# T5 attention and hash-routed experts in one kernel: zero fills, expert 0's head and the last chunk rescheduled

## The chip, the cores and the metric

One core of one Trainium2 chip. The metric is the device time of one execution in microseconds (us). The kernel before was timed three times; one more execution was taken with the profiler.

## What is computed

Attention with a relative-position bias over 8 batches of 8 heads, 576 positions of 64 values, then a mixture of 8 experts over the 4608 token rows of 512 values. A token's id decides its expert, so the assignment is known early, but its row of x is known only when attention has made it.

```python
scores = q @ k.transpose(0, 1, 3, 2) / sqrt(64) + bias_table[bucket]   # 8x8x576x576
attn   = softmax(scores)
x      = (attn @ v) as rows of 512                                     # 4608 rows
expert_idx = token_ids * 2654435761 % 8
for e in range(8):
    out[rows of e] = relu(x[rows of e] @ w1[e]) @ w2[e]                # 512 -> 1024 -> 512
```

## The kernel before

**Attention.** The work is 32 pairs of heads (`pairs`, four to a batch), each in five steps g = 0 to 4. For each step TensorE (PE) makes the scores of a pair in a PSUM slot (`products`, L475, and `add_bias`, L498; three slots, L174), ScalarE (ACT) takes their exponential into `att` (`scores`, L533), and the sum with v runs seven steps behind (`av_steps`, L601, nine matmuls a step, into the PSUM banks `aux0` and `aux1`). VectorE (DVE) multiplies two of the five `att` parts by a band factor (L543), divides the finished sums into `x_all` (L610, L611), copies the transposed k and q out of `aux1` (`transpose_qk`, L404 and L410) and casts v (`cast_v`, L252). GpSimd (POOL) casts q and k (L244).

**The order is written out by hand.** The loop at L853 takes the steps two at a time; `pair_start` (L784) issues what belongs to a pair's start, `behind` (L816) what comes after the scores. Each engine and each queue runs its instructions in that order and waits where an operand is not there. SyncE's queue (SP) issues the loads of q, k and v (L206, L220, L232), the routing's tables at pair 3, and the zero fills; POOL's queue issues the scatters and the weights' loads.

**From attention to the experts.** Expert e has 640 rows of a table `t_xperm` in device memory. `fill_table` (L746) writes zero rows with no token's id into the last 192 rows of each expert's share, 192 rows of 1028 bytes by one transfer, two experts a pair in pairs 4 to 7 (L794). From pair 10 on `send` lets POOL scatter finished rows of `x_all` to their places (`dispatch`, L625, five scatters a batch, two, two and one a pair). `route` (L306) works out the places and sets a flag where a count is out of bounds, so that a fallback behind the main part computes all rows.

**Heads.** The first 384 rows (`EARLY` x 128) of experts 0 and 1 are full before the last two batches, so they are read back early: `gather_head(0)` at the start of pair 29 into `xpn[0]`, `gather_head(1)` at the start of pair 31 (both L153, on SP). Weights of experts 0 and 1 are loaded by POOL at the starts of pairs 24, 26, 28 and 30 (`load_w1`, L140, and `load_w2`, L146), 1 MB each as they land. After the last pair `first_transpose` (L754, matmuls L760) transposes expert 0's head in a PSUM slot by 12 matmuls and one copy (L765), and 63 matmuls of the last two pairs' sums are left: 18 of pair 30, then 27 and 18 of pair 31.

**Experts.** The second part has pools of its own (`mo`, and `mop` in PSUM). Its parts (`PARTS`, L68) are the heads of experts 0 and 1, the rests of both, then experts 2 to 7 whole. For each, `first_layer` (L951 or L931) and a ReLU on ACT, then for each chunk of 128 rows `second_layer`: eight matmuls of 512 columns (L979), a copy by DVE (L985) and a scatter to the output (L986). The transposes of a later part stand between the chunks (`transpose_step`, L908 and L913).

Of the kernel before, what the change touches and what calls it, by code (L numbers as in the profile page):

```python
# [11 lines left out]
F32 = mybir.dt.float32  # L12
# [19 lines left out]
def kernel(  # L32
# [35 lines left out]
    PARTS = [(0, 0, EARLY), (1, 0, EARLY), (0, EARLY, NSC), (1, EARLY, NSC)]  # L68
    PARTS += [(e, 0, NSC) for e in range(2, E)]
    HEAD = (B - 2, B - 1)  # L70
    NPT = DM // P
    NFT = F // P
    NIT = 2 * NT + 1
# [25 lines left out]
    for t in range(NIT):  # L99
        for b in range(B):  # L100
# [22 lines left out]
    flag = cst.tile([1, 1], I32, name="flag")  # L123
    x_all = cst.tile([P, NRING, NIT, XW], F16, name="x_all")
    xpn = [cst.tile([P, c1 - c0, XW], F16, name=f"xpn_{e}_{c0}")
           for e, c0, c1 in PARTS[:4]]
    xpt0 = cst.tile([P, NPT, EARLY * P], F16, name="xpt0")
    w1t = [cst.tile([P, NPT, F], F16, name=f"w1t{i}") for i in range(2)]
    w2t = [cst.tile([P, NFT, DM], F16, name=f"w2t{i}") for i in range(2)]

# [35 lines left out]
    with tc.tile_pool(name="at", bufs=1) as at, tc.tile_pool(  # L166
# [139 lines left out]
        def route():  # L306
            name_rows(0, NRING)
            nc.vector.tensor_scalar(
                out=te[:, :, :KT].rearrange("p b (o t) -> p b o t", o=2),
                in0=ter[:, :, :, ::2].rearrange("p b t o -> p b o t"),  # L310
                scalar1=E - 1, scalar2=None, op0=ALU.bitwise_and,
            )
            nc.vector.tensor_scalar(
                out=te[:RC, :, KT:], in0=te[:RC, :, KT:], scalar1=E - 1,
                scalar2=None, op0=ALU.bitwise_and,
            )
            yield
            EN = E * NGT
            tef = te[:, :, :].rearrange("p b t -> p (b t)")
            oh = at.tile([P, E, NGT], F16, name="oh")  # L320
            nc.vector.tensor_tensor(
                out=oh[:, :, :],
                in0=tef.unsqueeze(1).to_broadcast([P, E, NGT]),
                in1=csts[:, NGT:].bitcast(F32).unsqueeze(2).to_broadcast(
                    [P, E, NGT]
                ),
                op=ALU.is_equal,
            )
            yield
            ohf = oh[:, :, :].rearrange("p e g -> p (e g)")  # L330
            rps = slot("rps")
            nc.tensor.matmul(out=rps[:, 0, :EN], lhsT=cnt[:, P:], rhs=ohf)
            nc.tensor.matmul(out=rps[:, 1, :EN], lhsT=cnt[:, :P], rhs=ohf)
            inc = at.tile([P, E, NGT], F32, name="inc")
            incf = inc[:, :, :].rearrange("p e g -> p (e g)")
            nc.vector.tensor_tensor_scan(
                out=incf, data0=keep[:, :, :].rearrange("p e g -> p (e g)"),
                data1=rps[:, 0, :EN], initial=0.0, op0=ALU.mult, op1=ALU.add,
            )
            yield  # L340
            rnk = at.tile([P, E, NGT], F32, name="rnk")
            rnkf = rnk[:, :, :].rearrange("p e g -> p (e g)")
            nc.vector.tensor_tensor(
                out=rnkf, in0=incf, in1=rps[:, 1, :EN], op=ALU.subtract
            )
            yield
            nc.vector.tensor_tensor(out=rnkf, in0=rnkf, in1=ohf, op=ALU.mult)
            yield
            rank = at.tile([P, NGT], F32, name="rank")
            nc.vector.tensor_reduce(  # L350
                out=rank[:, :], in_=rnk[:, :, :].transpose([0, 2, 1]),
                axis=mybir.AxisListType.X, op=ALU.add,
            )
            yield
            num = inc[:, :, NGT - 1]
            odd = at.tile([P, E + 2], F32, name="odd")
            nc.vector.tensor_scalar(
                out=odd[:, :E], in0=num, scalar1=float(LOW), scalar2=None,
                op0=ALU.is_lt,
            )  # L360
            nc.vector.scalar_tensor_tensor(
                out=odd[:, :E], in0=num, scalar=float(CAP), in1=odd[:, :E],
                op0=ALU.is_gt, op1=ALU.max,
            )
            yield
            for i, b in enumerate(HEAD):
                nc.vector.tensor_scalar(
                    out=odd[:, E + i : E + i + 1],
                    in0=inc[:, i, b * NIT - 1 : b * NIT],
                    scalar1=float(EARLY * P), scalar2=None, op0=ALU.is_lt,  # L370
                )
            bad = at.tile([P, 1], F32, name="bad")
            nc.vector.tensor_reduce(
                out=bad[:, :], in_=odd[:, :], axis=mybir.AxisListType.X,
                op=ALU.max,
            )
            yield
            sel = at.tile([P, NGT], F32, name="sel")
            nc.vector.scalar_tensor_tensor(
                out=sel[:, :], in0=tef, scalar=float(CAP), in1=rank[:, :],  # L380
                op0=ALU.mult, op1=ALU.add,
            )
            dlt = at.tile([P, NGT], F32, name="dlt")
            nc.vector.scalar_tensor_tensor(
                out=dlt[:, :], in0=tok, scalar=float(NSLOT),
                in1=sel[:, :], op0=ALU.add, op1=ALU.subtract,
            )
            yield
            nc.vector.scalar_tensor_tensor(
                out=ds2[:, :], in0=dlt[:, :], scalar=bad[:, :],  # L390
                in1=sel[:, :], op0=ALU.mult, op1=ALU.add,
            )
            nc.vector.tensor_copy(out=flag[:, :], in_=bad[:1, :])
            yield
# [230 lines left out]
        def dispatch(b, t):  # L625
# [8 lines left out]
                oob_is_err=False,  # L634
            )
            disjoint(sc_in, "xrows")
            for b0, read in heads:
                if b >= b0:
                    tc.declare_no_dep(
                        sc_in.ins, read.ins,  # L640
                        reason="the first rows of the list are of earlier "
                        "batches, or every row goes behind the lists",
                    )

        heads = []

        def gather_head(i):
            heads.append((HEAD[i], gather(i, xpn[i])))
# [96 lines left out]

        def fill_table(e):  # L746
            rows = CAP - LOW
            nc.sync.dma_start(
                out=xperm_d.ap()[CAP * (e + 1) - rows : CAP * (e + 1), :]
                .rearrange("(p r) d -> p (r d)", p=rows // 2),  # L750
                in_=zx[: rows // 2, :, :].rearrange("p r d -> p (r d)"),
            )

        def first_transpose():  # L754
            ps = slot("xp0")[:, :, :].bitcast(F16)
            w = EARLY * P
            for i in range(2):
                for j in range(NPT // 2):
                    for sc in range(EARLY):
                        nc.tensor.transpose(  # L760
                            out=ps[:, i, w * j + P * sc : w * j + P * sc + P],
                            in_=xpn[0][:, sc, ts(i * NPT // 2 + j, P)],
                            identity=ident[:, :],
                        )
            nc.vector.tensor_copy(  # L765
                out=xpt0[:, :, :].rearrange("p (i k) n -> p i (k n)", i=2),
                in_=ps[:, :, : w * NPT // 2],
            )

        NP = len(pairs)  # L770
# [13 lines left out]
        def pair_start(n):  # L784
# [6 lines left out]
                load(n // 2 + 2, "v")  # L791
            if n == 3:
                route_load()
            if 4 <= n < 4 + E // 2:  # L794
                fill_table(2 * (n - 4))
                fill_table(2 * (n - 4) + 1)
            if n + 3 < NP:
                cast_qk(n + 3)
            if b + 1 < B and m == 3:
# [16 lines left out]
        def behind(n, g):  # L816
# [7 lines left out]
                transpose_qk(n + 1)  # L824
            if g == 3 and 0 < n < NP - 2:
                transpose_qk(n + 2)
            if (m, g) == (3, 0) and b + 1 < B:
                transpose_rest(b + 1)
            if g == 2 and n + 1 < NP:
# [24 lines left out]
        for i in range(0, len(order), 2):  # L854
# [17 lines left out]
            for n, g in order[i + 2 : i + 3]:  # L872
                if g > 1:
                    add_bias(n, g, True)
        first_transpose()
        advance(av, 999)
        assert not waiting
        guard.__exit__(None, None, None)

    with tc.tile_pool(name="mo", bufs=1) as mo, tc.tile_pool(  # L880
# [3 lines left out]
            E_ALL.PE, E_ALL.Activation, E_ALL.Pool, E_ALL.SP, E_ALL.DVE,  # L884
        })
        guard.__enter__()
        xn, xt, hs, ids = dict(enumerate(xpn)), {0: xpt0}, {}, {}

        def load_rows(i):
            if i >= len(xpn):  # L890
                xn[i] = mo.tile([P, NSC, XW], F16, name="xpn", bufs=4)
            gather(i, xn[i])

        def width(i):
            return PARTS[i][2] - PARTS[i][1]

        def transpose_step(i, step):
            nsc = width(i)
# [68 lines left out]
        def second_layer(i, sc):  # L967
            e = PARTS[i][0]
            if sc == 0:
# [3 lines left out]
                    in0=xn[i][:, :, DM:XW].bitcast(I32), scalar1=NOID,  # L973
                    scalar2=None, op0=ALU.bitwise_and,
                )
            ops = mop.tile([P, DM], F32, name="ops", bufs=2,
                           space=bass.MemoryType.PSUM)
            for ft in range(NFT):
                nc.tensor.matmul(  # L979
                    out=ops[:, :], lhsT=hs[i][:, ft, ts(sc, P)],  # L980
                    rhs=w2t[e % 2][:, ft, :],
                    start=(ft == 0), stop=(ft == NFT - 1),
                )
            ok = mo.tile([P, DM], F32, name="ok", bufs=8)
            nc.vector.tensor_copy(out=ok[:, :], in_=ops[:, :])  # L985
            so = nc.gpsimd.indirect_dma_start(  # L986
                out=out[:, :],
                out_offset=bass.IndirectOffsetOnAxis(
# [20 lines left out]
        for i, (e, c0, c1) in enumerate(PARTS):  # L1009
            after = e + 2 if c1 == NSC and e + 2 < E else None  # L1010
            if e > 1 and i + 2 < len(PARTS):
                load_rows(i + 2)
            first_layer(i)
            if after:
                load_w1(after)
            for sc in range(c1 - c0):
# [128 lines left out]
```

## Time and profile before

| | us |
|---|---|
| median of three timed runs | 347.08 (345.6 to 350.08) |
| the profiled execution, its own time | 349.28 |
| its span, first to last instruction | 347.5 |
| mean granted TensorE clock | 0.982 of full speed |

Times in rows are microseconds from the span's start. The profiled execution lies 2.2 us over the median of the timed runs. A line of the profile is a line of the kernel, such as L533. A bracket behind a row tells how long its engine had been idle before it, and what ended that.

### The profile page before, as it was taken

The page shows a single profiled execution, that of the slowest core. Times are in us where ns is not written, and L with a number is a line of the kernel's source. Part 1 is how long each engine was busy: PE and PEld are TensorE (multiplying, and loading weights), DVE is VectorE, ACT ScalarE, POOL GpSimd, SP SyncE. Part 2 cuts the span into 40 slices and gives each one's busy share as a digit, 9 for nine tenths or more (in the row PEclk, how much of TensorE's full clock was granted, in tenths as well). Part 3 has the DMA queues.
Part 4 walks back from the last instruction along what each step waited for, and adds up shares of the span by engine and source line. Part 5 has one row for each costly group of instructions (what it writes and reads, how often), then busy time and mean ns, then how long its engine had stood idle before and what let it go on. Part 6 is the DMA issues. An engine that isn't in the chain of part 4 may idle for free.

```text
span 347.5 us, 8903 instructions
## 1 busy us (share of the span) xinstructions
PE 311.4 (90%) x3680; PEld 200.2 (58%) x3680; DVE 168.3 (48%) x391; ACT 203.7 (59%) x239; POOL 150.0 (43%) x202
## 2 busy tenths in 40 slices
PE   3569889997999999999998999999999999999980
PEld 1136565675667666766666556665656666565630
DVE  1214589875788878878765213313223231404030
ACT  2368979899599999999994232242322324150600
POOL 6042332434856667648562413433434251505050
PEclk9989999999899999999999999999999999999996
DMA  5989976969896979797897594999998979983030
GB/s 158 212 225 233 262 146 181 269 176 300 248 313 187 320 204 308 207 204 141 150 221 143 159 345 124 200 207 251 294 211 206 161 207 146 220 135 121 14 125 28
DMA packets 90786, 69.15 MB, mean 199 GB/s; under 512 B 11975, under 2 KB 82407, under 8 KB 90736
## 3 DMA queue, kind: packets, MB, share of 16 engines
q0 software_dynamic: 17664, 30.96, 41.3%
q1 hardware_dynamic: 72416, 37.16, 40.2%
q8 instruction: 31, 0.51, 0.6%
q10 hardware_dynamic: 656, 0.36, 0.4%
q14 instruction: 19, 0.16, 0.1%
HBM read 69.47 MB, written 17.35 MB: 250 GB/s over the span
## 4 chain that ended last, share of the span: by engine, by line
PE 72%; DMA 11%; DVE 6%; ACT 6%; issue 1%; POOL 1%; SPq 0%; POOLq 0%; DVEq 0%; ACTq 0%
PE ops L979 19%; PE hps L931 15%; PE px L601 10%; PE ps L491 8%; PE ps L468 7%; ACT att L533 5%; PE hps L951 5%; DMA vf<-in_v_dram 4%; PE pqk L404 4%; DMA kf<-in_k_dram 3%; DMA btb<-t_f 3%; PE xps L908 2%; PE ps L525 2%; DVE kq L410 1%; DVE att L543 1%
## 5 line engine op out<-in xcount | busy, mean ns | idle before, releaser
L533 ACT ACTIVATE att<-ps 128x1024 f16<-128x1024 f32 x160 | 151.2, 1059 | 21.4 <-PE ps L491 18.0
L985 DVE COPY ok<-ops 128x512 f32<-128x512 f32 x40 | 27.7, 691 | 109.0 <-PE ops L979 109.0
L937 ACT ACTIVATE h<-hps 128x640 f16<-128x640 f32 x48 | 33.8, 704 | 71.9 <-PE hps L931 71.9
L979 PE MATMUL ops<-w2t,h 128*128 128x512 f16 x320 | 75.1, 379 | 0.5 <-ACT h L959 0.5
L986 POOL DMA_INDIRECT out_dram<-ok,ids x40 | 39.5, 987 | 66.6 <-DVE ok L985 54.1
L601 PEld LDWEIGHTS <-att 128*128 128x128 f16 x1408 | 55.8, 98 | 18.8 <-issue 14.0
L601 PE MATMUL px<-va,att 128*128 128x65 f16 x1280 | 59.5, 194 | 4.9 <-DVE kq L410 4.3
L931 PE MATMUL hps<-xpt,w1t 128*128 128x320 f16 x384 | 53.3, 299 | 0.5 <-DVE xpt L913 0.5
L468 PE MATMUL ps<-btb,idents 128*128 128x384 f16 (+1 forms) x256 | 46.8, 268 | 6.3 <-DMA btb<-t_f 6.1
L491 PE MATMUL ps<-kq 64*128 64x512 f16 x256 | 44.9, 391 | 6.2 <-ACT att L533 5.0
L626 POOL DMA_INDIRECT t_xperm<-x_all,ds x40 | 41.5, 1037 | 20.7 <-DVE x_all L611 10.4
L979 PEld LDWEIGHTS <-h 128*128 128x128 f16 x320 | 30.1, 98 | 31.3 <-ACT h L959 1.5
L931 PEld LDWEIGHTS <-w1t 128*128 128x128 f16 x384 | 37.5, 98 | 16.0 <-issue 0.7
L543 DVE TENSOR_TENSOR att<-att,ebd 128x768 f16<-128x768 f16 x64 | 41.8, 654 | 7.1 <-ACT ebd L566 7.1
L244 POOL CAST qh<-qf 128x512 f16<-128x512 f32 x31 | 19.6, 632 | 51.0 <-PE pqk L404 22.2
L410 DVE COPY kq<-pqk 128x1024 f16<-128x1024 f16 x32 | 22.1, 690 | 27.7 <-PE pqk L404 27.7
L491 PEld LDWEIGHTS <-kq 64*128 64x128 f16 x512 | 17.1, 95 | 29.2 <-issue 20.2
L611 DVE TENSOR_TENSOR x_all<-px,rcp 128x384 f16<-128x384 f32 x64 | 31.4, 491 | 2.2
L468 PEld LDWEIGHTS <-idents 128*128 128x128 f16 x336 | 21.1, 99 | 18.4 <-issue 12.9
L244 POOL CAST kh<-kf 128x512 f16<-128x512 f32 x31 | 22.5, 726 | 11.6 <-DMA kf<-in_k_dram 11.6
L959 ACT ACTIVATE h<-hps 128x768 f16<-128x768 f32 (+1 forms) x12 | 10.6, 881 | 27.5 <-PE hps L951 27.5
L951 PE MATMUL hps<-xpt,w1t 128*128 128x384 f16 (+1 forms) x128 | 18.0, 299 | 0.8 <-DVE x_all L611 0.8
(85 smaller groups left out, 277.3 us busy)
## 6 DMA issues: line engine op xcount, KB each, us to landing
w1t<-in_moe_w_dram POOLq DMA_DIRECT2D x8, 1024.0 KB, 10.4
w2t<-in_moe_w_dram POOLq DMA_DIRECT2D x8, 1024.0 KB, 10.2
qf<-in_q_dram SPq DMA_DIRECT2D x30, 256.0 KB, 4.4
kf<-in_k_dram SPq DMA_DIRECT2D x30, 256.0 KB, 6.9
vf<-in_v_dram SPq DMA_DIRECT2D x30, 256.0 KB, 6.4
xpn<-t_xperm SPq DMA_DIRECT2D x6, 642.5 KB, 10.0
t_xperm<-zx SPq DMA_DIRECT2D x8, 192.8 KB, 6.1
btb<-t_f SPq DMA_DIRECT2D x3, 384.0 KB
```

Of the source, the lines that this page charges most:

```text
L244: (eng or nc.gpsimd).tensor_copy(out=dst[n][:, :, :, :].transpose([0, 2, 1, 3]), in_=src[n // 2][:, 2 * (n % 2) : 2 * (n % 2) + 2].rearran ...
L468: nc.tensor.matmul(out=out, lhsT=idents[:, which, :], rhs=rhs, start=start, stop=True, skip_group_check=True,)
L491: nc.tensor.matmul(out=ps[:, hh, o : o + rhs.shape[1]], lhsT=lhsT, rhs=rhs, start=not biased and (g < KT or t == 0), stop=True, skip_group ...
L533: nc.scalar.activation(out=att[:, g, :, :], in_=ps[:, :, :], func=AF.Exp, bias=0.0, scale=scale,)
L543: nc.vector.tensor_tensor(out=a, in0=a, in1=ebd[:, 2 * m : 2 * m + 2, 1 - c : 3 - c, :], op=ALU.mult,)
L601: nc.tensor.matmul(out=po, lhsT=lhsT, rhs=rhs, start=(i == 0), stop=(i == len(todo) - 1), skip_group_check=True,)
L626: sc_in = nc.gpsimd.indirect_dma_start(out=xperm_d.ap()[:, :], out_offset=bass.IndirectOffsetOnAxis(ap=ds2[:, NIT * b + t : NIT * b + t + ...
L931: nc.tensor.matmul(out=hps[:, nr, : n // 2], lhsT=w[:, kt, ts(ft, P)], rhs=xt[i][:, kt, ts(nr, n // 2)], start=(kt == 0), stop=(kt == NPT ...
L937: nc.scalar.activation(out=hs[i][:, ft, :].rearrange("p (r n) -> p r n", r=2), in_=hps[:, :, : n // 2], func=AF.Relu, bias=0.0, scale=1.0,)
L951: nc.tensor.matmul(out=hps[:, f // per, n * (f % per) : n * (f % per) + n], lhsT=w[:, kt, ts(f0 + f, P)], rhs=xt[i][:, kt, :], start=(f % ...
L979: nc.tensor.matmul(out=ops[:, :], lhsT=hs[i][:, ft, ts(sc, P)], rhs=w2t[e % 2][:, ft, :], start=(ft == 0), stop=(ft == NFT - 1),)
L986: so = nc.gpsimd.indirect_dma_start(out=out[:, :], out_offset=bass.IndirectOffsetOnAxis(ap=ids[i][:, sc, :], axis=0), in_=ok[:, :], in_off ...
```

## The change

Three edits, and what they need:

- The zero fills move from pairs 4 to 7 (two a pair) to pairs 11 to 18 (one a pair). The scatters of batches 0 to 3 and the fills are declared to need no order; a further flag sends all rows to the fallback if an expert had more than 448 tokens in those batches.
- Expert 0's head is transposed in two halves of six matmuls, behind step 3 of pairs 30 and 31, in bank `aux1`, each with a copy of its own. Its first layer is cut into four quarters, made in the attention's PSUM slots, one behind each 18, 27 and 18 matmuls of the sums that are left, and the last one behind all of them. The buffers of the two rests move from the constant pool to `mo`.
- The very last chunk's second layer is made in two halves of 256 columns, each with its own copy.

```diff
+    LEAD = B // 2
     xpn = [cst.tile([P, c1 - c0, XW], F16, name=f"xpn_{e}_{c0}")
-           for e, c0, c1 in PARTS[:4]]
+           for e, c0, c1 in PARTS[:2]]
+    h0 = cst.tile([P, NFT, EARLY * P], F16, name="h0")
+            nc.vector.tensor_scalar(
+                out=odd[:, E : 2 * E], in0=inc[:, :, LEAD * NIT - 1],
+                scalar1=float(LOW), scalar2=None, op0=ALU.is_gt,
+            )
             disjoint(sc_in, "xrows")
+            if b < LEAD:
+                lead.append(sc_in)
+                for fill in fills:
+                    apart(sc_in, fill)
         def fill_table(e):
...
-        def first_transpose():
-            ps = slot("xp0")[:, :, :].bitcast(F16)
...
+            for sc_in in lead:
+                apart(fill, sc_in)
+            fills.append(fill)
+
+        def head_transpose(i):
+            ps = aux(1, [P, NPT // 2, EARLY * P], F16, "xp0")
+            for j in range(NPT // 2):
+                for sc in range(EARLY):
+                    nc.tensor.transpose(
+                        out=ps[:, j, ts(sc, P)],
+                        in_=xpn[0][:, sc, ts(i * NPT // 2 + j, P)],
+                        identity=ident[:, :],
+                    )
             nc.vector.tensor_copy(
...
+        def head_layer(i):
+            hps = slot("hps0")
+            for f in range(2):
+                for kt in range(NPT):
+                    nc.tensor.matmul(
+                        out=hps[:, f, : EARLY * P],
+                        lhsT=w1t[0][:, kt, ts(2 * i + f, P)],
+                        rhs=xpt0[:, kt, :],
+                        start=(kt == 0), stop=(kt == NPT - 1),
+                    )
+            nc.scalar.activation(
+                out=h0[:, 2 * i : 2 * i + 2, :], in_=hps[:, :, : EARLY * P],
+                func=AF.Relu, bias=0.0, scale=1.0,
             )
-            if 4 <= n < 4 + E // 2:
-                fill_table(2 * (n - 4))
-                fill_table(2 * (n - 4) + 1)
+            if 11 <= n < 11 + E:
+                fill_table(n - 11)
+            if g == 3 and n >= NP - 2:
+                head_transpose(n - NP + 2)
-        first_transpose()
-        advance(av, 999)
+        for i, count in enumerate((18, 27, 18, 0)):
+            advance(av, count)
+            head_layer(i)
+            w = DM // 2 if (i, sc) == (len(PARTS) - 1, NSC - 1) else DM
+            for d0 in range(0, DM, w):
...
-            first_layer(i)
+            if i > 0:
+                first_layer(i)
```

## Rows read from the trace of the kernel before

**Rows 1.** The page, part 2: DMA busy tenths, 40 slices of 8.7 us.
```profile
DMA  5989976969896979797897594999998979983030
```

**Rows 2.** The timeline of ACT, exponentials of pairs 12 to 19: start, length, count.
```profile
88.90 2.04 ACT L533 ACTIVATE att<-ps 128x1024 f16<-128x1024 f32 x2 [1.97 <-PE ps L491]
92.72 13.04 ACT L533 ACTIVATE att<-ps 128x1024 f16<-128x1024 f32 x14 [1.78 <-PE ps L491]
...
112.28 13.04 ACT L533 ACTIVATE att<-ps 128x1024 f16<-128x1024 f32 x14 [0.24 <-PE ps L491]
```

**Rows 3.** The timeline of DVE, the cast of v for pair 12.
```profile
86.37 0.43 DVE L252 CAST va<-vf 128x512 f16<-128x512 f32 x1 [3.95 <-DMA vf<-in_v_dram]
```

**Rows 4.** Line L748, the zero fills: ns minimum, median, maximum; first and last start.
```profile
L748 SPq DMA_DIRECT2D t_xperm<-zx x8: 419/710/902, 58.1 to 69.4; - x8
```

**Rows 5.** The timeline of SP's queue: start and length of the issuing.
```profile
78.57 2.83 SPq L206 DMA_DIRECT2D vf<-in_v_dram  x2
...
102.92 1.38 SPq L220 DMA_DIRECT2D qr<-in_q_dram  x2
```

**Rows 6.** DMA from 57 to 77 us: packets, MB, share of 16 engines.
```profile
DMA packets 7815, 4.91 MB, mean 245 GB/s; under 512 B 820, under 2 KB 7044, under 8 KB 7812
...
q1 hardware_dynamic: 7812, 4.87, 96.6%
```

**Rows 7.** The timeline of PE from 76 to 93 us.
```profile
87.45 0.64 PE L601 MATMUL px<-va,att 128*128 128x65 f16 x16 [2.34 <-DVE kq L410]
```

**Rows 8.** Busy time by stretch: PE, PEld, DVE, ACT, POOL; PEclk, DMA share, GB/s.
```profile
107.00:126.50 19.50, 18.85 (x337) 13.09 (x334) 15.62 (x37) 18.97 (x23) 13.77 (x17) 1.00 0.81 231
...
88.90:92.30 3.40, 3.40 (x38) 2.69 (x36) 1.94 (x5) 2.03 (x2) 2.65 (x4) 0.50 0.87 253
```

**Rows 9.** The timeline of PE from 172 to 232 us.
```profile
178.55 0.22 PE L468 MATMUL ps<-btb,idents 128*128 128x64 f16 x2
...
183.53 0.62 PE L601 MATMUL px<-va,att 128*128 128x65 f16 x15
...
184.15 0.83 PE L760 MATMUL xp<-idents,xpn 128*128 128x128 f16 x12
...
187.07 0.66 PE L601 MATMUL px<-va,att 128*128 128x65 f16 x16 [0.60 <-DVE x_all L611]
...
188.67 5.36 PE L951 MATMUL hps<-xpt,w1t 128*128 128x384 f16 x32 [0.83 <-DVE x_all L611]
193.87 1.89 PE L979 MATMUL ops<-w2t,h 128*128 128x512 f16 x8
```

**Rows 10.** The timeline of SP from 160 to 240 us; first of nine.
```profile
171.31 57.07 SPq L153 DMA_DIRECT2D xpn<-t_xperm  x9
```

**Rows 11.** DMA from 171.2 to 178.9 us: queues, and an issue with its landing.
```profile
q0 software_dynamic: 525, 1.07, 90.5%
q1 hardware_dynamic: 219, 0.23, 10.8%
...
w2t<-in_moe_w_dram POOLq DMA_DIRECT2D x1, 1024.0 KB, 11.5
```

**Rows 12.** DMA from 180.5 to 184.2 us: the only queue with packets.
```profile
q0 software_dynamic: 616, 0.63, 122.4%
```

**Rows 13.** The timeline of DVE from 170 to 232 us, three sizes of copy.
```profile
185.52 0.95 DVE L765 COPY xpt<-xp 128x1536 f16<-128x1536 f16 x1
...
188.10 0.42 DVE L611 TENSOR_TENSOR x_all<-px,rcp 128x256 f16<-128x256 f32 x1
...
196.41 0.55 DVE L913 COPY xpt<-xps 128x768 f16<-128x768 f16 x1
```

**Rows 14.** The timeline from 336 to 340 us, the last chunk's copy.
```profile
337.25 0.69 DVE L985 COPY ok<-ops 128x512 f32<-128x512 f32 x1 [1.03 <-PE ops L979]
```

**Rows 15.** The chain that ended last, from 205 to 232 us.
```profile
208.98 1.73 PE ops L979 x8
...
211.16 3.51 PE hps L951 x32
```

More of the change, by code (lines that the diff above doesn't have):

```diff
@@ L355, in route @@
             num = inc[:, :, NGT - 1]
-            odd = at.tile([P, E + 2], F32, name="odd")
+            odd = at.tile([P, 2 * E + 2], F32, name="odd")
             nc.vector.tensor_scalar(
@@ L365, in route @@
             yield
+            nc.vector.tensor_scalar(
+                out=odd[:, E : 2 * E], in0=inc[:, :, LEAD * NIT - 1],
+                scalar1=float(LOW), scalar2=None, op0=ALU.is_gt,
+            )
             for i, b in enumerate(HEAD):
                 nc.vector.tensor_scalar(
-                    out=odd[:, E + i : E + i + 1],
+                    out=odd[:, 2 * E + i : 2 * E + i + 1],
                     in0=inc[:, i, b * NIT - 1 : b * NIT],
@@ L643, in dispatch, with apart @@
                     )
-        heads = []
+        heads, lead, fills = [], [], []
+        def apart(later, earlier):
+            tc.declare_no_dep(
+                later.ins, earlier.ins,
+                reason="the first batches end ahead of the filled rows, or "
+                "every row goes behind the lists",
+            )
         def gather_head(i):
@@ L747, in fill_table @@
             rows = CAP - LOW
-            nc.sync.dma_start(
+            fill = nc.sync.dma_start(
                 out=xperm_d.ap()[CAP * (e + 1) - rows : CAP * (e + 1), :]
@@ L752, in fill_table @@
             )
-        def first_transpose():
-            ps = slot("xp0")[:, :, :].bitcast(F16)
[L756 to L764, printed above, removed]
-            nc.vector.tensor_copy(
-                out=xpt0[:, :, :].rearrange("p (i k) n -> p i (k n)", i=2),
-                in_=ps[:, :, : w * NPT // 2],
+            for sc_in in lead:
[10 more added lines that the diff above has]
+                    )
+            nc.vector.tensor_copy(
+                out=xpt0[:, i * NPT // 2 : (i + 1) * NPT // 2, :],
+                in_=ps[:, :, :],
+            )
+        def head_layer(i):
[7 more added lines that the diff above has]
+                        start=(kt == 0), stop=(kt == NPT - 1),
+                    )
+            nc.scalar.activation(
+                out=h0[:, 2 * i : 2 * i + 2, :], in_=hps[:, :, : EARLY * P],
+                func=AF.Relu, bias=0.0, scale=1.0,
             )
@@ L874 @@
                     add_bias(n, g, True)
-        first_transpose()
-        advance(av, 999)
+        for i, count in enumerate((18, 27, 18, 0)):
+            advance(av, count)
+            head_layer(i)
+        assert next(av, "end") == "end"
         assert not waiting
@@ L886, with width @@
         guard.__enter__()
-        xn, xt, hs, ids = dict(enumerate(xpn)), {0: xpt0}, {}, {}
+        xn, xt, hs, ids = dict(enumerate(xpn)), {0: xpt0}, {0: h0}, {}
+        def width(i):
+            return PARTS[i][2] - PARTS[i][1]
         def load_rows(i):
             if i >= len(xpn):
-                xn[i] = mo.tile([P, NSC, XW], F16, name="xpn", bufs=4)
+                xn[i] = mo.tile([P, width(i), XW], F16,
+                                name=f"xpn{width(i)}",
+                                bufs=4 if width(i) == NSC else 2)
             gather(i, xn[i])
-        def width(i):
-            return PARTS[i][2] - PARTS[i][1]
         def transpose_step(i, step):
@@ L975, in second_layer @@
                 )
[L976 to L982, printed above, removed]
-                )
-            ok = mo.tile([P, DM], F32, name="ok", bufs=8)
-            nc.vector.tensor_copy(out=ok[:, :], in_=ops[:, :])
+            ok = mo.tile([P, DM], F32, name="ok", bufs=8)
+            w = DM // 2 if (i, sc) == (len(PARTS) - 1, NSC - 1) else DM
+            for d0 in range(0, DM, w):
+                ops = mop.tile([P, DM], F32, name="ops", bufs=2,
+                               space=bass.MemoryType.PSUM)
+                for ft in range(NFT):
+                    nc.tensor.matmul(
+                        out=ops[:, :w], lhsT=hs[i][:, ft, ts(sc, P)],
+                        rhs=w2t[e % 2][:, ft, d0 : d0 + w],
+                        start=(ft == 0), stop=(ft == NFT - 1),
+                    )
+                nc.vector.tensor_copy(
+                    out=ok[:, d0 : d0 + w], in_=ops[:, :w]
+                )
             so = nc.gpsimd.indirect_dma_start(
```

## The prediction, made before the changed kernel was run

> **What bounds the kernel now.** I read the page first, for where DMA is dense, then the timeline of each engine around the places that the diff touches, then the queues. DMA stands at eight and nine tenths from the third slice almost to the end [rows 1], so a transfer that is moved is taken from one crowded stretch and put into another; whether it costs anything hangs on who waits there. In the attention the paced engine is ACT. Its exponentials follow each other closely, and the idle time that the timeline shows in batch 4 is 0.24 us at its first pair [rows 2]. At the same place in batch 3, pair 12, it is 1.97 and then 1.78 us [rows 2]. That is the one large hole after pair 8, and the first edit aims at it. Behind the last pair PE sets the end: sums, first layer and second layers follow one another, with two idle pieces of 0.60 and 0.83 us [rows 9].
>
> **The hole at pair 12, and the fills.** Followed back, ACT waits for PE's scores, PE idles 2.34 us for DVE [rows 7], and DVE stands 3.95 us before the cast of v, waiting for that load [rows 3]. SP issued the load at 78.57 [rows 5]. Ahead of it in SP's queue stand the eight fills. They cost twice. Their issuing is 8 x 0.71 = 5.7 us of SP's time, between 58.1 and 70 us [rows 4]. And they move 8 x 192 rows x 1028 bytes = 1.58 MB, which at the 245 GB/s of that stretch is 6.4 us of DMA; nearly all that moved there is SP's own queue, at 96.6% of the engines [rows 6], so what follows a fill lands later by the fill's whole time. Without them the v load should land 5.7 to 6.4 us earlier. It was late by 3.95 us, so the wait goes, with about 2 us to spare. What is late next at that place is nothing that the rows show: the same pair of batch 4 has its 0.24 us. The gain is 1.97 + 1.78 - 0.24 = 3.5 us. Part of it is PE's clock: behind the idle 2.34 us the granted clock fell to 0.50, the 1.2 GHz level, from 88.9 to 92.3 us [rows 8], and ACT's second wait lies in that stretch. Bounds: nothing gained, if the load waits for something else too, and 3.75 if the rest of the idle time goes with it.
>
> **The fills at their new place.** Pairs 11 to 18 take one each. SP then issues 0.71 us more a pair, and the loads queued behind a fill move by that much. DMA gets 4 x 0.197 MB in four pairs, 0.79 MB, some 3.2 us at 245 GB/s in a stretch of 19.5 us; that stretch now has a share of 0.81 [rows 8], so 0.97 after. That is close to full but not over it, and SP is ahead there: the loads that belong to pair 16 begin at 102.92 [rows 5], while that pair's last exponential starts at 112.28 and its first about four lengths of 0.93 us (13.04 / 14) earlier, near 108.5 [rows 2]. I cost this at nothing. If the cover is gone, a v load is late again, and the price is that of the old hole, 3.5 us. The scatters that no longer wait for fills had found them done, so this part of the edit moves nothing. The flag's additional DVE operation is of the order of the smallest ones, some 0.2 us at most, at pairs 7 and 8; I leave it out.
>
> **The head's transposes.** Behind step 3 of pair 30 stand now six transposes of `xpn[0]`. In the old order PE is there at 178.55, where the bias of the next step begins [rows 9]. The gather of these rows was issued at 171.31 [rows 10]. Has it landed by 178.55? The queue view says no. From 171.2 to 178.9 SP's queue, on which this gather is the only transfer, moved 0.23 MB of its 0.39, beside 1.07 MB of POOL's queue (weights and scatters) [rows 11]. From 180.5 on SP's queue moves nothing [rows 12]. So its last bytes move after 178.9 and before 180.5, and it had landed by 184.15, where the old transposes ran without a wait [rows 9]. The weights issued in the same stretch took 11.5 us from issue to landing [rows 11]; the gather stands behind such a load as well, so I take 11.5 for it too: 171.31 + 11.5 = 182.8. PE then waits 182.8 - 178.55 = 4.25 us. Bounds are 180.5 - 178.55 = 1.95 and 184.15 - 178.55 = 5.6 us. The old place, 5.6 us later, hid this landing; the new one doesn't. All that PE has queued behind the transposes waits with it: the scores of pair 30's last step and of pair 31, hence six exponentials, the sums, and the quarters of the first layer. DVE, ACT and the last scatters follow PE. Nothing can go around them in PE's order. Earlier pairs that end 3.5 us sooner don't help, since gather, weights and transposes all move with the pairs.
>
> The Trainium skill, in DMA: Bandwidth & Descriptors (section "Queues, rings and completion order"), says that each DMA engine takes the queue rows that have work in turn, packet by packet. By that a gather would not stand behind a weight load at all; the 0.23 MB against 1.07 MB [rows 11] don't look like taking turns in equal bytes, so I don't follow it. By that rule the sum would be -5.2 us, by the rows it is the one below.
>
> **PE's clock behind the wait.** An idle time of 4.25 us is longer than the 2.34 us behind which the clock fell to 0.50 [rows 7, 8]. I expect the same stretch of about 3.4 us at 1.2 GHz. It cost ACT 1.78 - 0.24 = 1.5 us there [rows 2], and here PE sets the end, so I take 1.5 (bounds 0, if it stays at 2.4 GHz, and 3.4, if two such stretches follow).
>
> **The tail.** From 183.53 to 193.87 the old order spends 10.34 us [rows 9]: sums, 12 transposes (0.83 us with their last drain), sums, 0.60 idle, sums, 0.83 idle, 5.2 us of first layer. Three things change. Half of the transposes, 0.4 us, leave this stretch; the other half stays. The 0.83 us before the first layer (its PSUM waits for the last `x_all`) lies beside the last two quarters, 2.6 us of PE's work. The 0.60 us came from DVE, where the 0.95 us copy stood ahead of a sum's release [rows 13]; the copy is now in halves of 768 columns, 0.55 us by an equal one [rows 13], but `aux1` is wanted by the next sums, so PE waits some 0.4 us there. Gain 0.4 + 0.83 + 0.60 - 0.4 = 1.4 us, between 0.5 (if the second layer's PSUM waits for the last ReLU) and 1.8. The batch-7 scatters start later against PE by up to two quarters, 2.6 us; the rests that need them are transposed only at the fourth chunk of the second part, and I cost that at nothing. The moved buffers of the rests cost nothing either, as their gathers wait for those scatters anyhow.
>
> **The last chunk.** Eight matmuls of 512 columns take 1.73 us; sixteen of 256 take half of 3.51, 1.75 [rows 15]. The copy behind the last one falls from 0.69 [rows 14] to that of 256 columns, 0.42 by the nearest row [rows 13]. Gain 0.3 us.
>
> **Sum.** -3.5 (fills) + 4.25 (wait for the gather) + 1.5 (clock) - 1.4 (tail) - 0.3 (last chunk) = +0.5 us. On the profiled execution's own 349.28 that is 349.8; it lies 2.2 us over the median of the runs, and on that median, 347.08, it is 347.6.
>
> **Rivals.**
> *The gather is there in time.* It needs to land 7.2 us after issue. The queue view speaks against it [rows 11]. Then no wait and no fall of the clock: -3.5 - 1.4 - 0.3 = -5.2, 341.9 us. The Trainium skill's rule of taking turns, in the page and section named above, would give this one. Chance 0.2, as other executions may place the weights otherwise.
> *A short wait, full clock.* The lower bound of 1.95 us and no fall: -3.5 + 1.95 - 1.4 - 0.3 = -3.25, 343.8. Chance 0.2.
> *Slower: a fill makes a v load late again in pairs 11 to 18.* The price is one hole of 3.5 us, and it decides as soon as the load of some pair lands later than DVE's cast; for it speaks the share of 0.97 worked out above, against it SP's lead of some 5 us. Then 0 + 4.25 + 1.5 - 1.4 - 0.3 = +4.05 against before, 351.1. Chance 0.1.
> *The fills' move does nothing for pair 12* (the load is late for the other transfers ahead of it): the same sum, 351.1. Against it speak 5.7 us of issuing against 3.95 us of lateness. Chance 0.05.
> The forecast has 0.45.
>
> **How the numbers follow.** The forecast's own range, with the wait between 3 and 5.6 and the clock's price between 0 and 3.4, is 345 to 351. The range takes in the rivals down to the gather in time: 341.5 to 351. A measurement of this kernel can tell about 2% from no change, 6.9 us. Faster by more than that needs more than all gains together, 5.2 us: 0.08. Slower by more needs a second hole and two falls of the clock: 0.03. Within 2%: 0.89.
>
> **What would show it.** In the changed kernel ACT's exponentials of pair 12 should follow with about 0.24 us of idle time, and the clock stay at 1.00 there. PE should stand before the first transposes of pair 30, with the gather's DMA as what ended it, some 4 us, and a stretch at 0.50 should begin during or right after it. The first matmul of the second layer should start about 0.85 us later than before (-3.5 + 4.25 + 1.5 - 1.4). The forecast is wrong if PE doesn't wait before the transposes, if the hole at pair 12 is still there, or if a new one stands in pairs 13 to 20.

## The result, and the profile after

The changed kernel takes 349.06 us in the median (347.10 to 351.92, 20 runs), the kernel before beside it 347.46 (344.68 to 350.08, 20 runs): ratio 1.0052, 95% interval 1.0030 to 1.0073. That is no change by the 2% bound, 1.5 us above the forecast and inside its range. The profiled execution took 348.82 us with a span of 346.94 us, that of before 349.28 and 347.48. Ratios, and the median given for `e2_head_alone` below, leave out executions over 1.5% above the fastest of their kernel (three of twelve there, the profiled one among them). Beneath the small difference lie large ones of both signs. The table cuts the spans at the first exponential of a pair on ACT and the second layer's first matmul on PE (us):

| stretch | before | after | difference |
|---|---|---|---|
| start to pair 5 | 49.24 | 45.51 | -3.73 |
| pairs 5 to 11 | 35.75 | 35.76 | +0.01 |
| pair 12 | 8.65 | 4.81 | -3.84 |
| pairs 13 to 29 | 82.57 | 82.16 | -0.41 |
| pair 30 to the second layer | 17.66 | 25.62 | +7.96 |
| second layer to the end | 153.61 | 153.09 | -0.52 |

The hole at pair 12 is gone. The timeline of DVE has the cast that stood 3.95 us in [rows 3] without a wait:

```profile
83.66 0.42 DVE L254 CAST va<-vf 128x512 f16<-128x512 f32 x1
```

The wait has moved to the early transposes. First the timeline of PE, then of ACT, of SP's queue and of POOL:

```profile
176.73 0.82 PE L778 MATMUL xp<-idents,xpn 128*128 128x128 f16 x6 [6.00 <-DMA xpn<-t_xperm]
...
178.67 1.94 ACT L539 ACTIVATE att<-ps 128x1024 f16<-128x1024 f32 x2 [6.61 <-PE ps L497]
...
166.65 15.98 SPq L155 DMA_DIRECT2D xpn<-t_xperm  x2
...
157.79 0.40 POOL L276 CAST vt<-vr 64x256 f16<-64x256 f32 x1 [2.87 <-DMA vf<-in_v_dram]
```

PE is through with the work ahead of the transposes at 176.73 - 6.00 = 170.73, only 4.1 us after SP issued the gather; in [rows 9, 10] the same distance was 178.55 - 171.31 = 7.2 us. POOL tells a part of why: it stands 2.87 us before the cast of the last batch's v rest, and the scatters that the gather needs are queued behind that cast. In the profile of before POOL had no wait there. What POOL waited for isn't told: the row names a load of v that the cast doesn't read, and its own load was issued by 139.6. The last scatter that the gather needs, before and after:

```profile
168.80 1.01 POOL L626 DMA_INDIRECT t_xperm<-x_all,ds  x1 [0.31 <-issue]
...
162.66 0.97 POOL L632 DMA_INDIRECT t_xperm<-x_all,ds  x1 [0.31 <-issue]
```

From this scatter PE had 9.75 us to the place of the transposes before (178.55) and has 8.07 after (170.73): 1.7 us less. From the scatter to the gather's issue 2.51 us passed before and 3.99 after: 1.5 us more, for which the rows name no reason.

From issue to release the gather took 10.1 us. The queues in this time (packets, MB, share of 16 engines), then in its first 2.4 us, 166.6 to 169, and from 171.5 to 174:

```profile
q0 software_dynamic: 984, 1.70, 95.9%
q1 hardware_dynamic: 400, 0.39, 15.0%
...
q0 software_dynamic: 230, 0.47, 109.7%
...
q0 software_dynamic: 231, 0.53, 73.5%
q1 hardware_dynamic: 229, 0.24, 30.2%
```

The gather is queue q1, POOL's weights and scatters are q0; in the first 2.4 us q1 has no row. The clock by stretch (PE, PEld, DVE, ACT, POOL; PEclk, DMA share, GB/s):

```profile
175.90:182.70 6.80, 5.97 (x62) 3.93 (x63) 2.27 (x6) 3.58 (x4) 0.00 (x0) 0.50 0.84 148
```

The clock stood at 0.50, the 1.2 GHz level, for 6.8 us, two stretches of the length seen in [rows 8]. Last, the tail on PE and the copy that ends the last chunk:

```profile
185.51 0.64 PE L607 MATMUL px<-va,att 128*128 128x65 f16 x16 [0.30 <-DVE xpt L783]
...
190.19 2.76 PE L792 MATMUL hps<-xpt,w1t 128*128 128x384 f16 x16
193.85 1.89 PE L1020 MATMUL ops<-w2t,h 128*128 128x512 f16 x8 [0.90 <-ACT h L798]
...
337.32 0.42 DVE L1025 COPY ok<-ops 128x256 f32<-128x256 f32 x1 [0.52 <-PE ops L1020]
```

The 0.83 us in front of the first layer [rows 9] have become 0.90 us in front of the second one, which the last ReLU ends; whether the second layer waits for its PSUM or for `h` isn't told.

### The profile page after: what moved, and what is told of

The parts are those of the page before. It is cut to its first block, busy times and chain, and to the rows that moved or that the text cites. A ratio compares the mean times of both kernels' runs of the same rounds, so it can differ in the third digit from the quotient of the medians.

```text
span 346.9 us, 8921 instructions
## 1 busy us (share of the span) xinstructions
PE 312.3 (90%) x3688; PEld 201.1 (58%) x3688; DVE 169.0 (49%) x394; ACT 203.7 (59%) x239; POOL 151.3 (44%) x202
## 4 chain that ended last, share of the span: by engine, by line
PE 74%; DMA 10%; ACT 6%; DVE 5%; issue 1%; POOL 0%; POOLq 0%; SPq 0%; ACTq 0%; DVEq 0%
PE ops L1020 20%; PE hps L969 15%; PE px L607 10%; PE ps L497 8%; PE ps L474 7%; ACT att L539 5%; PE pqk L410 4%; PE hps L989 4%; DMA kf<-in_k_dram 3%; DMA xpn<-t_xperm 3%; DMA btb<-t_f 3%; PE xps L946 2%; PE ps L531 2%; PE hps L792 2%; DMA t_xperm<-x_all,ds 1%
## 5 line engine op out<-in xcount | busy, mean ns | idle before, releaser
L1025 DVE COPY ok<-ops 128x512 f32<-128x512 f32 (+1 forms) x41 | 27.8, 679 | 106.2 <-PE ops L1020 106.2
L1020 PE MATMUL ops<-w2t,h 128*128 128x512 f16 (+1 forms) x328 | 75.2, 374 | 1.4 <-ACT h L798 0.9
L1020 PEld LDWEIGHTS <-h 128*128 128x128 f16 x328 | 30.8, 98 | 31.9 <-ACT h L997 1.5
L997 ACT ACTIVATE h<-hps 128x768 f16<-128x768 f32 (+1 forms) x8 | 7.3, 916 | 22.5 <-PE hps L989 22.5
L142 POOL DMA_DIRECT2D w1t<-in_moe_w_dram x8 | 6.5, 808 | 28.5 <-PE hps L969 25.1
```

The lines of the kernel that those rows point to most:

```text
L1020: nc.tensor.matmul(out=ops[:, :w], lhsT=hs[i][:, ft, ts(sc, P)], rhs=w2t[e % 2][:, ft, d0 : d0 + w], start=(ft == 0), stop=(ft == NFT - 1),)
```

## The experiments

Theory A, the prediction's, is that the fills' gain pays for a wait on the gather. Its rivals are that the early gather costs little, that the wait is repaid later anyhow, and that the hole at pair 12 belongs to single executions; from group 2 on B is the rival named in the run's own expectation. Theory C, with D against it, came up on the way: it is about the first row of the table, where no edit lies. Four groups of runs were made, each on another chip; ratios are to runs of the kernel before in the same group.

**Group 1: the parts.** The kernel before takes 353.99 us here. `e1_fills_alone` is the kernel before with the fills' edit:

```diff
-            if 4 <= n < 4 + E // 2:
-                fill_table(2 * (n - 4))
-                fill_table(2 * (n - 4) + 1)
+            if 11 <= n < 11 + E:
+                fill_table(n - 11)
```

> Only the fills move (and the flag's operation comes with them); expert 0's head and the last chunk stay as before. If the fills ahead of the v load made the hole at pair 12, it is gone here and nothing replaces it: 3.5 to 4 us less than before, some 343.5 us. If the fills only trade one crowded stretch for another, the hole comes back in pairs 13 to 20 and the time is within 1 us of before.

Measured: 353.24 us, ratio 0.9990 (0.9958 to 1.0022). No gain. `e2_head_alone` is the changed kernel with this edit taken back (a memset stands for the flag's operation).

> Only the head's transposes and quarters and the halved last chunk; the fills stay at pairs 4 to 7. If PE's wait for the gather at pair 30 is the cost, this is slower than before by 4 to 6 us, some 352 us, with PE idle before the first transposes and the clock at 0.50 behind it. If the wait is only there because the fills' move hurried the pairs past a DMA that can't follow, PE waits clearly less here than the 6.00 us of the changed kernel, and the time is within 2 us of before.

Measured: 354.32 us, ratio 1.0009 (0.9966 to 1.0051), within 2 us of before as the second reading said. It doesn't decide between the two: on a chip this slow the whole change costs no time either (`f1_after` below). `e3_late_transposes` is the changed kernel with the transposes at their old place and the quarters kept:

```diff
-            if g == 3 and n >= NP - 2:
-                head_transpose(n - NP + 2)
...
+        first_transpose()
         for i, count in enumerate((18, 27, 18, 0)):
```

> The changed kernel with all 12 transposes of the head behind the last pair, where they stood before; the four quarters of the first layer stay among the last sums. If the place of the transposes is the cost, PE's wait and the half clock go and the gain of the fills is kept: 5 to 8 us less than the changed kernel, some 342.5 us. If the quarters among the sums are the cost (last scatters later, PSUM waiting for the last ReLU), the time stays within 2 us of the changed kernel.

Measured: 354.28 us, ratio 1.0019 (0.9987 to 1.0051). The changed kernel itself did not run in this group, so what the expectations of `e3` and `e4` say against it stays open here. `e4_late_weights` is the changed kernel with expert 1's two weight loads issued at pairs 30 and 31 in place of 28 and 30:

```diff
-            if n >= 24 and n % 2 == 0:
-                (load_w1 if n % 4 == 0 else load_w2)((n - 24) // 4)
+            if n in (24, 26, 30, 31):
+                (load_w1 if n in (24, 30) else load_w2)((n - 24) // 4)
```

> The changed kernel with expert 1's two weight loads issued at pairs 30 and 31 in place of 28 and 30, so behind the head's gather. If the gather is late because it shares the DMA engines with the first of these loads, it lands some 4 us after its issue in place of 10, PE's wait before the transposes is under 2 us and the time falls by 4 to 7 us against the changed kernel, to some 343.5 us. If the gather is late because the scatters that it waits for are late, it is issued no earlier and lands no sooner, and the time stays.

Measured: 351.99 us, ratio 0.9956 (0.9923 to 0.9989), the only one of the four that is faster than before. Neither `e3` nor `e4` waits for the gather, and both have another wait, longer than the 0.90 us above. PE ahead of the second layer, in `e4`:

```profile
197.41 1.89 PE L1020 MATMUL ops<-w2t,h 128*128 128x512 f16 x8 [2.52 <-ACT h L798]
```

**Group 2: before, after, a part and the late weights again.** The kernel before takes 353.06 us. `f0_before` is the kernel before itself.

> The kernel before, unchanged, timed against itself and profiled on the chip of this group. Both theories: ratio 1.00 (within 0.998 to 1.002). What it tells: how long pair 12 is in its profile on this chip. Theory A (the fills' zero rows crowd the DMA engines and make a v load late): pair 12 is 2 to 4 us longer than its neighbours of the same kind, with a DVE cast that waits for a v load. Theory B (that hole belongs to single executions): pair 12 is at most 1 us longer.

Measured: 352.81 us, ratio 0.9994 (0.9969 to 1.0019). Pair 12 takes 5.42 us instead of 8.65, within theory B's 1 us. The same cast on DVE:

```profile
83.74 0.45 DVE L252 CAST va<-vf 128x512 f16<-128x512 f32 x1 [1.65 <-DMA vf<-in_v_dram]
```

The load is late here too, but by 1.65 us, and PE hardly waits for it. Pairs 13 to 29 take 88.9 us in this profile against 82.57: with slower pairs a load has more time. What slows them isn't shown.

> The changed kernel again, beside its parts on one chip. Theory A (the fills' move gives back what the early gather costs): ratio 1.002 to 1.008, TensorE idle 4 to 6 us ahead of the first transposes with the gather as releaser, and a clock of 0.50 for one or two stretches behind it. Theory B (the early transposes cost little when the pairs run slower, since the gather then has more time): idle under 3.5 us and a ratio of 0.997 to 1.002.

Measured: 352.65 us, ratio 0.9979 (0.9959 to 0.9999), inside B's bands for both the ratio and the idle time. Its waits on PE, and SP's queue:

```profile
181.88 0.82 PE L778 MATMUL xp<-idents,xpn 128*128 128x128 f16 x6 [2.18 <-DMA xpn<-t_xperm]
...
198.66 1.67 PE L1020 MATMUL ops<-w2t,h 128*128 128x512 f16 x7 [1.73 <-ACT h L798]
...
170.79 16.80 SPq L155 DMA_DIRECT2D xpn<-t_xperm  x2
```

The gather took 11.1 us, but PE had 8.9 us of other work (181.88 - 2.18 - 170.79), so 2.18 were left. Issue to release is nearly the same on both chips; what PE has to do meanwhile is not. Here POOL doesn't wait before the cast of the v rest (0.06 us).

> Only the fills moved (and the flag that goes with them), again. Theory A: where the kernel before of this group has the hole at pair 12, this one lacks it and is 2 to 3.5 us faster (ratio 0.990 to 0.994). Theory B: ratio 0.997 to 1.001, as the first time, whatever the profile of before shows at pair 12.

Measured: 352.61 us, ratio 0.9985 (0.9959 to 1.0011). No gain again; there was hardly a hole to remove.

> The changed kernel with expert 1's two weight loads issued at pairs 30 and 31, behind the head's gather, in place of 28 and 30. Theory A: the gather lands within 4 us, no idle ahead of the transposes, full clock; 3 to 6 us faster than the changed kernel beside it. Theory B (the wait is repaid later, since the weights land later and the second part starts no earlier): within 1.5 us of the changed kernel.

Measured: 349.86 us, ratio 0.9919 (0.9894 to 0.9945), 2.8 us faster than the changed kernel beside it. SP's issue, PE's rows, and the queue while the gather moves, from 169.8 to 172.4 us:

```profile
169.82 15.62 SPq L155 DMA_DIRECT2D xpn<-t_xperm  x2
...
179.34 0.50 PE L778 MATMUL xp<-idents,xpn 128*128 128x128 f16 x6 [0.49 <-DVE x_all L617]
...
194.76 1.89 PE L1020 MATMUL ops<-w2t,h 128*128 128x512 f16 x8 [1.80 <-ACT h L798]
```
```profile
q1 hardware_dynamic: 399, 0.39, 47.2%
```

Nothing but the gather and one packet of instructions moves, and 2.6 us after its issue at 169.82 the gather is through. The weights beside it made the difference between 2.6 and 10 or 11 us, and the later weights aren't repaid: from the second layer to the end this profile takes 153.30 us, f1's 152.85, that of before 153.91. PE doesn't wait for the gather, and the clock doesn't fall there. Theory A holds, its size somewhat below the 3 us that it gave as the least.

In the result's profile (the queues' rows in the first section) none of the gather's packets moved in the first 2.4 us, beside 230 of the weights' and scatters' queue; the first came 3.9 us after the issue, in `f3` 1.0 us after it. From 171.5 to 174 us 229 moved beside 231, and from there to 176.7 149 beside 365. The Trainium skill (DMA: Bandwidth & Descriptors, "Queues, rings and completion order") has each DMA engine take turns among the queues' packets. The stretch from 171.5 to 174 agrees with it, the others do not, and the rule as the prediction used it did not bring the gather in time. What held the first packets back isn't shown.

**Group 3: the first row.** The kernel before takes 346.96 us. Pair 5 starts at 45.5 to 46.6 us in all profiles so far with the head's edits, at 47.9 to 50.1 in all without, though between `f2` and `f3`, for one, no instruction ahead of it differs. What differs is the place of the tiles in SBUF. The head's edits drop two `xpn` tiles and add `h0`; all that is allocated behind moves up by 1,984 bytes. In the compiled programs the k stage `kf` begins 64 bytes past a multiple of 512 before, and on such a multiple after; so does the band table's tile `btb`, while the q and v stages begin on no multiple of 256 in either. `g2_shift_alone` is the kernel before with one line more:

```diff
     xpt0 = cst.tile([P, NPT, EARLY * P], F16, name="xpt0")
+    shift = cst.tile([P, 992], F16, name="shift")
```

> The kernel before with one unused tile of 1,984 bytes per partition behind xpt0, which puts all later tiles where the changed kernel has them (two tiles of gathered rows less, h0 more, add up to that shift); no instruction differs. Six profiles with the head's edits start pair 5 at 45.5 to 46.6 us, four without at 47.9 to 50.1. Theory C (the tiles' places set how fast the first loads come): pair 5 starts at 45.5 to 46.6 us, 1.5 to 2.7 us faster than before, ratio 0.992 to 0.996. Theory D (the early difference is chance, or of something else): pair 5 at 47.5 to 50 us, ratio 0.998 to 1.002.

Measured: 343.78 us, ratio 0.9923 (0.9890 to 0.9956), 2.7 us faster than before with no instruction changed. Pair 5 starts at 47.20, between the two bands, and pair 12 takes 6.15. This gain is in the ratios of `e2`, `e3`, `e4`, `f1` and `f3` too, which all have the new place; it is not in the 2.8 us between `f1` and `f3`. `g3_late_weights_64` is `f3` with 64 bytes more behind `h0` (a tile of `[P, 32]`), which puts `kf` back to 64 bytes past such a multiple.

> The kernel with late weights and an unused tile of 64 bytes per partition behind h0, which gives all later tiles the same place within 512 bytes as in the kernel before. Theory C (it is the place within 512 bytes): pair 5 starts at 47.5 to 50 us, and most of the gain is gone: ratio 0.997 to 1.001. Theory D: pair 5 at 45.5 to 46.6 us and a ratio of 0.991 to 0.996, as without the tile.

Measured: 342.81 us, ratio 0.9908 (0.9875 to 0.9941). Pair 5 starts at 47.70, as theory C said; the ratio is theory D's. C's band for the ratio had taken all of `f3`'s gain for the place, and it is only part. The row that decides is SP's queue from 30 to 40 us, in `f0_before`, `g3`, `g2` and `g1` (packets, MB, share of 16 engines):

```profile
q1 hardware_dynamic: 4545, 2.09, 76.6%
```
```profile
q1 hardware_dynamic: 4643, 2.13, 80.3%
```
```profile
q1 hardware_dynamic: 5135, 2.39, 84.8%
```
```profile
q1 hardware_dynamic: 5119, 2.40, 84.1%
```

The first two have the old place, the last two the new one. Over all profiles, six with the old place moved 2.09 to 2.16 MB in these 10 us and eight with the new one 2.29 to 2.40; pair 5 starts at 47.70 to 50.21 and at 45.41 to 47.20. That the place matters is shown, by `g2`. Which tile does it, and whether other places are better still, was not tried. The Trainium skill (DMA: Bandwidth & Descriptors, "How a descriptor splits into AXI transactions") says that each transaction of a descriptor starts at a 256-byte boundary. By that page, an estimate, a 512-byte row of the k loads is two transactions on the new place and three on the old one. The rows agree with it in sign. No run here shows whether it is the reason: the page speaks of reads, and it is the written side that moved.

`g1_quarters_first` is `f3` with the last two quarters ahead of the last sums:

```diff
-        for i, count in enumerate((18, 27, 18, 0)):
+        for i, count in enumerate((18, 27, 0, 0)):
             advance(av, count)
             head_layer(i)
+        advance(av, 18)
```

> The kernel with late weights, and the last two quarters of the first layer both ahead of the last 18 AV products (counts 18, 27, 0, 0 and then 18). Theory A (the second layer's first matmul waits for the last ReLU, and the AV products can hide that): TensorE's idle ahead of the second layer falls from 1.8 us to about 1.1, 0.6 us faster than with late weights alone (ratio to before 0.990 to 0.994). Theory B (something else sets that start, since it stood at 197.41 us in two kernels whose pairs ended 1.1 us apart): the second layer starts no earlier, and the last scatters go out 1.3 us later, so 0 to 1 us slower than late weights alone (0.992 to 0.998).

Measured: 340.85 us, ratio 0.9860 (0.9813 to 0.9907), the fastest of all and below the bands of both theories. PE:

```profile
179.32 4.06 PE L792 MATMUL hps<-xpt,w1t 128*128 128x384 f16 x24
184.76 1.89 PE L1021 MATMUL ops<-w2t,h 128*128 128x512 f16 x8 [0.78 <-ACT h L798]
```

The wait ahead of the second layer is 0.78 us against 0.90 in `g3` beside it, and from pair 30 to the second layer `g1` takes 16.97 us, `g3` 17.08. So the order of the quarters is worth 0.1 us on this chip, and most of the 2.0 us between the two medians is the place, by which pair 5 starts at 45.41 us here and at 47.70 in `g3`.

**Group 4: the fills once more.** The kernel before takes 347.11 us, so the pairs are quick.

> Only the fills moved, a third time. So far: no gain where the kernel before took 353 to 354 us and its pairs 13 to 29 ran some 5.2 us each, and no hole at pair 12 in its profile there (5.42 us); a hole of 4 us in the profile of before where it took 347 us and these pairs 4.9 us each. Theory A (the fills cost time only where the pairs are fast enough for the v load to be late): if before takes 346 to 348 us here, pair 12 is under 5 us and the ratio 0.987 to 0.993; if it takes 352 to 354 us, 0.997 to 1.001. Theory B (the hole belongs to single executions): 0.997 to 1.001 in either case.

Measured: 344.63 us, ratio 0.9947 (0.9915 to 0.9980): 1.8 us gained, less than A's band and more than B's. Pair 12 takes 4.69 us. Two rows, of PE and of POOL, show what can have taken the rest:

```profile
182.66 0.84 PE L779 MATMUL xp<-idents,xpn 128*128 128x128 f16 x12 [1.15 <-DMA xpn<-t_xperm]
...
163.75 0.40 POOL L275 CAST vt<-vr 64x256 f16<-64x256 f32 x1 [3.66 <-DMA t_xperm<-x_all,ds]
```

Even at the old place PE now waits for the gather. POOL stands 3.66 us before the cast of the last batch's v rest (this row names a scatter as what ended the wait, that of the result a v load), and scatters and gather come later against the pairs, as in the profile of the result. The other profiles bear this out. Where the pairs are quick and POOL waits there (the result, `h1`, `g3`, `g1`), pair 12 takes 4.69 to 4.81 us and PE is at the place of the early transposes 4.1 to 5.3 us after the gather's issue. Where they are quick and it doesn't (before, `g2`, both with the fills at pairs 4 to 7), pair 12 takes 8.65 and 6.15 us and that distance is 7.2 and 7.1 us. In the eight profiles of the slower groups POOL doesn't wait there (0.06 us), with the fills at either place. How long pair 12 was before on this chip isn't known: a hole as small as `g2`'s is another reading of the 1.8 us. And the first pairs took 50.21 us in this execution, 1.0 more than in that of before.

## Why the prediction was right, and where not

The verdict and the range were right. That the sum came out near the measured time is in part luck: four of its terms were off and one was missing, and their errors have both signs.

**The hole at pair 12** went as worked out in the profile, -3.84 us against -3.5, and the fills' new place made no v load late for DVE, none of whose casts of v waits after 40 us: the share of 0.97 was not too much. Over all profiles pair 12 takes 5.42 to 8.65 us with the fills at their old place and 4.53 to 5.61 with them moved. As a term for the median it was too large. It was read from one execution; 0.9947 on quick pairs is -1.8 us, 0.9990 and 0.9985 on slower ones -0.4 and -0.5, not told from nothing. The step that failed is "What is late next at that place is nothing that the rows show": the place was looked at, the rest of the kernel not. Late next, where the pairs are quick, is POOL's cast in the last batch, with the scatters and the gather behind it.

**The wait for the gather** had the right place and releaser and nearly the right landing (11.5 forecast; 10.1 and 11.1 measured), and its size was 6.00 in the result and 2.18 in group 2 against 4.25. The step that failed is "Earlier pairs that end 3.5 us sooner don't help, since gather, weights and transposes all move with the pairs". They don't move alike: PE reached the transposes 4.1 us after the issue instead of 7.2. Of these 3.2 us 1.7 go with the scatters that POOL's wait held back and 1.5 with the slower way from the last scatter to the issue. The landing was 1.4 us quicker than forecast, so 4.25 + 3.2 - 1.4 is the measured 6.0.

**The clock** fell as said. From pair 30 to the second layer 7.96 us were lost. 6.00 are the wait; without wait and fall `g3` takes 17.08, 0.6 us less than the 17.66 of `g2` beside it and of before, so 7.96 - 6.00 + 0.6 = 2.6 us are the clock's, an estimate, against 1.5 taken and 3.4 as the upper bound: two stretches, not one. How long PE had waited doesn't tell alone whether the clock falls. Behind the 2.18 us in `f1_after` it did for one stretch, behind the 2.52 us in `e4` it did not:

```profile
181.80:185.20 3.40, 3.32 (x41) 2.55 (x42) 1.22 (x3) 1.39 (x2) 0.00 (x0) 0.50 1.21 209
...
197.40:200.80 3.40, 3.39 (x21) 1.73 (x21) 1.16 (x2) 0.00 (x0) 0.22 (x1) 1.00 0.18 38
```

**The tail** gained these 0.6 us, and not 1.4. That is near the bound of 0.5, in which the second layer waits for the last ReLU. On the slower chips that wait was 1.73 to 2.52 us and took all of the gain; why the last ReLU starts late there isn't shown.

**The last chunk.** From the second layer to the end six profiles with whole chunks take 152.88 to 154.10 us, mean 153.58; the six with a halved one and no fall of the clock behind it 152.78 to 153.30, mean 153.03. That is some 0.5 us, where 0.3 was said, with as much scatter between single profiles.

**The missing term** is the place of the tiles, 2.7 us by `g2` (1.5 to 3.8). The prediction says of the moved buffers that they "cost nothing", with only the gathers in mind. With it the result's parts are -2.7 (place) - 1.8 (fills) + 6.0 + 2.6 - 0.6 (tail) - 0.5 = +3.0 us, measured +1.8 (+1.0 to +2.5): the sizes come from different chips and executions, and their sum is off by about 1 us.

"About 0.85 us later" for the second layer's first matmul was 0.02 us earlier (193.85), by two errors that nearly cancel: the early start, 3.7 us, and the larger wait with its clock and the smaller gain of the tail, 3.6 us.

The prediction reads [rows 1] as eight and nine tenths almost to the end; the row has slices of four to seven tenths among them. No term rests on it.

## What to carry to other kernels

A hole that disappears moves everything behind it closer to its DMA: after costing a removed wait, walk on to each later in-order queue (here POOL's scatters behind a cast) and ask what it waits for when the pairs come earlier. A transfer that is wanted soon should not be issued beside large ones that nobody wants yet; holding two weight loads back by one or two pairs took the gather from 11.1 to 2.6 us at no later cost that shows. When an edit adds or drops a tile, compare where all later tiles begin.

## What was not expected of the hardware

An unused tile of 1,984 bytes made the kernel before 2.7 us faster (0.9923, 0.9890 to 0.9956). From 30 to 40 us SP's queue moved 2.39 MB with it, and 2.13 in `g3`, at the old place on the same chip. And the same program differs between groups by more than the whole change: 347 us in two of them, 353 to 354 in the other two, with the pairs 13 to 29 at 82 and 89 us. Each group had a chip and a time of its own, so which of the two makes the difference isn't shown.
